# Banded attention on one core: float16 pairs for two more tiles, and score products cut into quadrants of 64 by 64

## The chip, the cores and the metric

The kernel runs on one core of one Trainium2 chip. The metric is device time in microseconds (us) of one execution; less is better. The core has a matrix engine (TensorE, PE in the profile, with its weight loads as PEld), VectorE (DVE), ScalarE (ACT), GpSimd (POOL), SyncE (SP, which issues the DMAs here) and 16 DMA engines.

## The reference

Three stages in a row. Only the first is touched by the change: causal attention with a window of 128 positions and a bias that falls linearly with distance, over 4 batches, 8 heads, 576 positions and head size 64.

```python
scores = scale * np.matmul(q, k.transpose(0, 1, 3, 2))
rel = pos[:, None] - pos[None, :]
bias = slopes[:, None, None] * (-np.abs(rel).astype(np.float32))[None, :, :]
mask = (rel >= 0) & (rel < window)                # window = 128
scores = np.where(mask, scores + bias[None], -1e9)
attn = np.exp(scores - np.max(scores, axis=-1, keepdims=True))
attn = attn / (np.sum(attn, axis=-1, keepdims=True) + 1e-09)
x = np.matmul(attn, v)                            # then to 2304 tokens x 512
h = np.maximum(x @ w_in, 0.0)                     # dense layer, 512 -> 2048 -> 512
x = h * h @ w_out
# then a mixture of 8 experts (512 -> 1024 -> 512), gated by a Sinkhorn iteration
```

## The kernel before, in words

**Tiles.** The 2304 tokens are 18 tiles of 128. Each batch of 576 has four full tiles of 128 positions and 64 left over; the left-overs of two batches make one tail tile. So tiles 0 to 3 and 4 to 7 are full tiles of the first two batches, tile 8 is their tail, and tiles 9 to 17 are the same again. Because the window is 128, a full tile needs its own keys and those of the tile before it (none for tiles 0, 4, 9 and 13). A tail's two halves of 64 queries have different previous tiles.

**One tile of attention.** q and k are transposed on TensorE, so that two heads lie in the two halves of 64 partitions. `scores` multiplies them in float32, two heads (one index j) at a time, from tile 3 on for two values of j in one unit: lines 637 (own keys), 640 (a tail's previous keys, 64 queries at a time) and 642 (a full tile's previous keys). A float32 product shows as two matmul rows, two passes. VectorE adds the bias and takes the maximum (line 651), ScalarE the exponential (line 663). Then the exponentials must be turned before they can be multiplied with the values, and here tiles differ:
- tiles 0 to 8 stay in float32: `turn_e` transposes on TensorE (line 676), ScalarE copies the result back (line 681), `gather` multiplies with the raw values (line 698), two passes a product;
- tiles 9 to 17 (`paired`) are written as a float16 number and a float16 residual: ScalarE casts (`e_hi`, line 550), GpSimd subtracts (`e_lo`, line 437), a DMA transposes (`flip_e`, line 440), and `gather_pairs` makes three float16 matmuls where a float32 one was (line 580). Their values are split in the same way, with a common scale: `v_norm`, `v_sum`, `v_scale`, `v_hi` (line 529), `v_lo` (line 532), and `join_v` (line 545), which rescales a previous tile's values.

**After attention.** Tiles are handed to the dense layer in blocks of 4, 2, 4, 4 and 4. Its products h (line 1037) and y (line 1076) are float16 pairs as well, 96 and 96 matmuls a tile. Its weights come in four groups, which VectorE (lines 901 to 909 and 933) and ScalarE must unpack and split first. The experts follow (lines 1453 and 1548).

**Order.** The program is put in order by a planner (`Plan`): each unit of work has an engine, a cost in us, a rank, what it waits for and what buffers it takes and frees. The planner runs through time and lets each engine take the ready unit of least rank. Attention tiles have ranks by 100 times their number; h and y products have ranks above a million, so on TensorE they fill what attention leaves free. Up to 66 us by the planner's clock, TensorE gets small matmuls that compute nothing (`keep_warm`, line 319) where it has nothing else. GpSimd's units and some of VectorE's (the names in `PORT`, `e_lo` by its engine and `narrow`, `w_lo`, `v_lo` and `join_v` by name) are never planned at the same time, since they share a port. Splitting the values of tiles 9 to 17 (`v_hi`) waits for the first block's y to be done, whose memory it takes over.

Of the kernel before, what the change touches and what calls it, by code (L numbers as in the profile page):

```python
# [15 lines left out]
HI, LO = 0, 1  # L16
# [158 lines left out]
def kernel(  # L175
# [166 lines left out]
    def make_tail():  # L342
# [7 lines left out]

    plan = Plan(
        dict(
            raw=8, qT=2, kT=5, s=1, sp=1, diag=1, e=3, eh=2, eT=3, vo=4, vp=1, av=1, x=1, xh=1, x0=1, x1=1, xb=1, yacc=1,
            h=2, r=2, sq=4, ya=2, y=4, stage=4, scr=1, hp=24, t=10,
        ),
        ("raw", "qT", "kT", "e", "eh", "eT", "vo", "vp", "av", "x", "xh", "stage", "scr", "ya", "y"),
        Model({PE: 0.205, ACT: 0.16, DVE: 0.14, POOL: 0.1}, {PE: 0.0, ACT: 0.135, DVE: 0.115, POOL: 0.12}, 0.065, True),
    )
    GEMM, LATER = -1000000, 1000000
# [33 lines left out]
    def c_act(n, fixed=0.18):  # L393
        return fixed + n * 0.83e-3
# [113 lines left out]
    def v_scale(i):  # L508

        m = main[i]  # L510
        sc = scale_v[i] = small.tile([P, 2], F32, tag="sc", bufs=8, name=f"sc{i}")
        yield from pow2_of_norm((sc[:, 0:1],), m.pop("vss"), 1, WHOLE)
        for x in m["pv"]:
# [5 lines left out]
        for x in m["pv"]:  # L519
            yield  # L520
            f = tiny(1, "fs", bufs=6)
            DVE.tensor_tensor(out=f, in0=scale_v[x][:, 0:1], in1=sc[:, 1:2], op=ALU.mult)
            m["fs"].append(f)

    def v_hi(i):
        if "room" not in values:
            values["room"] = ap_.tile([P, 4, 2, H, D], F16, tag="yacc", name="values")
        values[i] = values["room"][:, plan.got["vo"]]
        ACT.activation(out=values[i][:, HI], in_=raw[i, 2], func=ACTF.Copy, scale=scale_v[i][:, 1:2])

    def v_lo(i):
        DVE.scalar_tensor_tensor(
            out=values[i][:, LO], in0=raw.pop((i, 2)), scalar=scale_v[i][:, 1:2], in1=values[i][:, HI], op0=ALU.mult,
            op1=ALU.subtract,
        )

# [27 lines left out]
    def gather_pairs(i, j):  # L564
        m = main[i]
        if j == 0:
            m["x"] = ps.tile([P, H, D], F32, tag="av", bufs=1, name=f"av{i}")
        eT = m.pop(("eT", j))
        tail = tiles[i][0] == "tail"
        everyone = slice(0, P)  # L570
        for n in range(2):
            h = 2 * j + n
            todo = [(everyone, eT.shape[3] - 1, values[i])]
            if tail:
                todo += [(g, 0, values[x]) for g, x in zip(halves(i), m["pv"])]
            elif m["pv"]:
                todo.append((everyone, 0, m["vp"]))
            for x, (r, c, v_) in enumerate(todo):
                for a, b in PAIRS:
                    PE.matmul(  # L580
                        m["x"][r, h, :], lhsT=eT[:, a, n, c, r], rhs=v_[:, b, h, :], start=x == 0 and a == b,
                        stop=x == len(todo) - 1 and a == LO, skip_group_check=tail,
                    )

    def start(i):
# [34 lines left out]
    def scores(i, js):  # L620

        m = main[i]
        if js[0] == 0:
            m["sum"] = tiny(H, "sum", bufs=3)
            m["nmax"] = tiny(H, "nmax", bufs=3)
        if in_ya(i, js[0]):
            sp = [pa_.tile([P, 512], F32, tag="ya", bufs=2, name=f"s{i}_{js[0]}_{n}") for n in range(2)]
        else:
            sp = pa_.tile([P, 2, 512], F32, tag="sp", bufs=1, name=f"s{i}_{js[0]}")
            sp = [sp[:, n] for n in range(2)]  # L630
        for x, j in enumerate(js):
            at = [sp[n][:, 2 * x * P : 2 * (x + 1) * P] for n in range(2)]
            m["s", j] = at
            for n in range(2):
                r = slice(n * D, (n + 1) * D)
                q_ = m["qT"][r, j]
                PE.matmul(at[n][:, P : 2 * P], lhsT=q_, rhs=keys[i][r, j], start=True, stop=True)  # L637
                if tiles[i][0] == "tail":
                    for g, y in zip(halves(i), m["pv"]):
                        PE.matmul(at[n][g, :P], lhsT=q_[:, g], rhs=keys[y][r, j], start=True, stop=True)  # L640
                elif m["pv"]:
# [41 lines left out]
    def gather(i, j):  # L683
        m = main[i]
        if j == 0:
            m["x"] = ps.tile([P, H, D], F32, tag="av", bufs=1, name=f"av{i}")
        eT = m.pop(("eT", j))
        tail = tiles[i][0] == "tail"
        everyone = slice(0, P)
        for n in range(2):  # L690
            h = 2 * j + n
            todo = [(everyone, eT.shape[2] - 1, i)]
            if tail:
                todo += [(g, 0, x) for g, x in zip(halves(i), m["pv"])]
            elif m["pv"]:
                todo.append((everyone, 0, i - 1))
            for x, (r, c, o) in enumerate(todo):
                PE.matmul(  # L698
                    m["x"][r, h, :], lhsT=eT[:, n, c, r], rhs=raw[o, 2][:, h, :], start=x == 0,
                    stop=x == len(todo) - 1, skip_group_check=tail,  # L700
                )

    done = {}
# [2 lines left out]
    def plan_tile(i):  # L706
# [18 lines left out]
            T.append((t, c))  # L725
        a["kT"], a["v"] = T[1], ld[2]
        jv = None
        if paired(i):
            n = len(pv)
            u = unit(ACT, c_act(W), v_norm, i, rank=z, after=[ld[2], st])  # L730
            mx = unit(
                PE, 0.3, v_sum, i, rank=z, take=["s"], after=[constants["ones"], u, *(done[p]["sc"] for p in pv)]
            )
# [5 lines left out]
            a["v"] = unit(DVE, c_dve(W, 1.17), v_lo, i, rank=z + 11, after=[vh])  # L739
            plan.free(ld[2], "raw", a["v"])  # L740
            if pv:
                older = [] if full else [x for p in pv for x in done[p]["uses"]]
                jv = unit(
                    DVE, 0.43 * n, join_v, i, rank=z + 6, take=["vp"] if full else [],
                    after=[*(done[p]["v"] for p in pv), a["sc"], *older],
                )
        S, X, G = [], [], []
        for j in range(H // 2):
            r = z + 10 * (j + 1)
            js = [j] if i < JOINED else [j, j + 1]  # L750
            if i < JOINED or j % 2 == 0:
                s = unit(
                    PE, 0.26 + 0.24 * nk + 0.9 * (len(pv) > 1) + (0 if i < JOINED else 0.22 * nk + 0.8 * (len(pv) > 1)), scores, i, js, rank=r, take=["ya", "ya"] if in_ya(i, j) else ["sp"],
                    after=[T[0][1], T[1][1], *(done[p]["kT"][1] for p in pv), *S[-1:]],
                )
            b = unit(DVE, 0.27 + 0.265 * nk, bias, i, j, rank=r, take=["e"], after=[s, constants["tail" if len(pv) > 1 else "band"]])
# [2 lines left out]
            if paired(i):  # L759
# [5 lines left out]
                f, cost = gather_pairs, 0.17 * nk + 0.48 * (len(pv) > 1)  # L765
            else:
                t = unit(PE, c_pe(4 * nk, P), turn_e, i, j, rank=r - 5, take=["s", "eT"], after=[x])
                plan.free(b, "e", t)
                c = unit(ACT, c_act(2 * P * nk, 0.07), turned_e, i, j, rank=r - 1, after=[t])
                plan.free(t, "s", c)  # L770
                f, cost = gather, 0.45 * nk
            g = unit(PE, cost, f, i, j, rank=r + 5, take=["av"] if j == 0 else [], after=[c, jv or a["v"], a["v"], *G[-1:]])
            plan.free(t, "eT", g)
            S.append(s)
            X.append(x)
# [2 lines left out]
        for p in (*pv, i):  # L778
            plan.free(done[p]["kT"][0], "kT", *S)
            if not paired(i):  # L780
                plan.free(done[p]["v"], "raw", *G)
            elif full and p != i:
                plan.free(done[p]["vo"], "vo", jv)
            else:
                plan.free(done[p]["vo"], "vo", *G)
        if full and jv:
            plan.free(jv, "vp", *G)
        a["uses"] = [*G, jv]
        z += 80
        st0, _, st = chain(DVE, [TINY, 0.12, 0.62], settle, i, rank=z, take=["x"], after=[*G, *X], port=(0,))  # L790
        plan.free(G[0], "av", st)
        nx = unit(ACT, c_act(W), x_norm, i, rank=z, after=[st])
# [1237 lines left out]
```

## Time and profile before

| | |
|---|---|
| median of 3 runs | 1885.62 us (1885.02 to 1885.77) |
| the profiled execution | 1885.8 us |
| its span, first to last instruction | 1884.0 us |
| mean granted TensorE clock | 0.997 |
| TensorE, VectorE, ScalarE, GpSimd busy | 99%, 80%, 66%, 47% |
| attention | ends at 372 us |

A matmul's row is longer than the array is occupied by it, since matmuls are pipelined: how much of TensorE's time an instruction takes is read from the distance between starts, not from its duration. The granted clock is 1.00 at 2.4 GHz and 0.50 at 1.2 GHz.

### The profile page before, as it was taken

To read this page: it belongs to the slowest core of one execution; us is meant where nothing else is said; L and a number is where in the kernel's file an instruction comes from. 1 tells how busy PE (TensorE), PEld (TensorE's weight loads), DVE (VectorE), ACT (ScalarE), POOL (GpSimd) and SP (SyncE) were. 2 spreads that over 40 slices of the span, in tenths; PEclk is the share of its full clock that TensorE was granted. 3 is DMA by queue.
4 is the path that set the end of the run, shared out by engine and by line. 5 is a ranking of instruction groups with operands and counts; after the bars stand their busy time and mean duration, and the time that the engine had idled before them with its cause. 6 is when DMAs were issued, how large, how long until landed. Compare 5 with 4: busy or idle time off the path is not lost.

```text
span 1884.0 us, 46737 instructions
## 1 busy us (share of the span) xinstructions
PE 1871.5 (99%) x18336; PEld 1676.5 (89%) x18336; DVE 1498.4 (80%) x3853; ACT 1236.2 (66%) x3434; POOL 890.3 (47%) x1182
## 2 busy tenths in 40 slices
PE   9999999999999999999999999999999999999999
PEld 9888888888889899888989989898988988888998
DVE  7996575354358988888898989888898988889876
ACT  6877486354358877666666666666666766666654
POOL 2322345258448744454445544454454535455432
PEclk9999999999999999999999999999999999999999
DMA  9555275110010111010100101010001001000002
GB/s 279 151 143 99 44 114 87 26 52 1 2 46 13 35 35 35 24 35 13 35 24 24 35 23 35 13 35 24 24 24 35 24 24 35 18 30 13 2 24 79
DMA packets 159660, 85.32 MB, mean 45 GB/s; under 512 B 112080, under 2 KB 144848, under 8 KB 159440
## 3 DMA queue, kind: packets, MB, share of 16 engines
q1 hardware_dynamic: 159360, 82.22, 17.4%
q8 instruction: 143, 2.34, 0.5%
q14 instruction: 77, 0.63, 0.1%
q10 hardware_dynamic: 80, 0.13, 0.0%
HBM read 64.50 MB, written 4.72 MB: 37 GB/s over the span
## 4 chain that ended last, share of the span: by engine, by line
PE 88%; DVE 6%; ACT 2%; DMA 2%; issue 1%; POOL 1%; SPq 0%; DVEq 0%; POOLq 0%; ACTq 0%
PE X L1453 19%; PE oX L1548 18%; PE oY L1548 9%; PE Y L1453 9%; PE h L1037 9%; PE y L1076 9%; PE oZ L1548 5%; PE Z L1453 5%; DVE hp L1529 1%; PE s L637 1%; DMA stage<-in_moe_w_dram 1%; PE av L698 1%; PE av L580 1%; PE t L599 1%; DVE acc_wc L1574 1%
## 5 line engine op out<-in xcount | busy, mean ns | idle before, releaser
L1453 PEld LDWEIGHTS <-late 128*128 128x128 f16 x6720 | 617.2, 98 | 71.4 <-issue 5.6
L1548 PEld LDWEIGHTS <-hp 128*128 128x128 f16 x6048 | 583.8, 98 | 64.0 <-issue 0.3
L1548 PE MATMUL oX<-late,hp 128*128 128x256 f16 x3456 | 468.3, 273 | 0.2 <-ACT acc_wd L1569 0.2
L1529 DVE TENSOR_TENSOR hp<-late,hp 128x256 f16<-128x256 f32 (+1 forms) x492 | 228.0, 471 | 21.6 <-ACT hp L1525 18.9
L1453 PE MATMUL Y<-y,late 128*128 128x256 f16 (+1 forms) x1920 | 241.4, 262 | 0.2 <-DVE hp L1508 0.2
L1548 PE MATMUL oY<-late,hp 128*128 128x256 f16 x1728 | 234.4, 273 | 0.0
L437 POOL TENSOR_TENSOR sq<-r,sq 128x256 f16<-128x256 f32 x144 | 107.9, 751 | 249.6 <-ACT sq L1062 245.3
L1525 ACT ACTIVATE hp<-late 128x256 f16<-128x256 f32 (+1 forms) x492 | 193.3, 396 | 46.9 <-POOL late L1515 26.5
L1076 PE MATMUL y<-sq,w_out 128*128 128x256 f16 x1728 | 216.1, 273 | 0.2 <-DVE y L1144 0.2
L1037 PE MATMUL h<-xT,w_in 128*128 128x256 f16 x1728 | 214.9, 274 | 0.3 <-DVE w_in L933 0.3
L1453 PE MATMUL X<-late 128*128 128x256 f16 (+1 forms) x1728 | 204.9, 255 | 2.1 <-ACT late L1481 0.6
L1037 PEld LDWEIGHTS <-w_in 128*128 128x128 f16 x1728 | 169.3, 99 | 21.0 <-DVE w_in L933 0.6
L1076 PEld LDWEIGHTS <-w_out 128*128 128x128 f16 x1728 | 166.9, 98 | 20.2 <-DVE y L1144 0.5
L437 POOL TENSOR_TENSOR stage<-stage 128x256 f32<-128x256 f32 x210 | 160.7, 765 | 34.2 <-DVE late L1353 27.9
L1495 ACT ACTIVATE late<-late 128x256 f32<-128x256 f32 (+1 forms) x202 | 78.5, 393 | 131.5 <-DVE late L1485 129.5
L1353 DVE SCALAR_TENSOR_TENSOR late<-stage,es,late 128x512 f16<-128x512 f32 (+2 forms) x180 | 154.6, 865 | 7.3 <-ACT late L1347 5.9
L1453 PE MATMUL X<-form,late 128*128 128x256 f16 x1152 | 157.1, 272 | 0.4 <-ACT late L1481 0.2
L1529 DVE TENSOR_TENSOR hp<-x,hp 128x256 f16<-128x256 f32 (+1 forms) x308 | 148.9, 489 | 10.7 <-ACT hp L1525 9.1
L1525 ACT ACTIVATE hp<-x 128x256 f16<-128x256 f32 (+1 forms) x308 | 121.7, 397 | 22.4 <-POOL x L1515 12.6
L1347 ACT ACTIVATE late<-stage,es 128x512 f16<-128x512 f32 (+2 forms) x180 | 135.5, 788 | 0.5 <-POOL stage L437 0.3
L1054 DVE SCALAR_TENSOR_TENSOR r<-h,unit_s,r 128x256 f32<-128x256 f32 x96 | 46.2, 482 | 112.3 <-ACT r L1046 112.0
L1515 POOL TENSOR_TENSOR late<-late 128x256 f32<-128x256 f32 (+1 forms) x57 | 45.4, 796 | 186.4 <-DVE hp L1529 178.3
(231 smaller groups left out, 3381.7 us busy)
## 6 DMA issues: line engine op xcount, KB each, us to landing
stage<-in_moe_w_dram SPq DMA_DIRECT2D x60, 256.0 KB, 3.1
stage<-in_moe_w_dram SPq DMA_DIRECT2D x30, 512.0 KB, 3.4
st_in<-in_moe_w_in_dram SPq DMA_DIRECT2D x16, 512.0 KB, 6.6
st_out<-in_moe_w_out_dram SPq DMA_DIRECT2D x16, 512.0 KB, 6.4
raw_q<-in_q_dram SPq DMA_DIRECT2D x16, 256.0 KB, 4.8
raw_k<-in_k_dram SPq DMA_DIRECT2D x16, 256.0 KB, 4.3
raw_v<-in_v_dram SPq DMA_DIRECT2D x16, 256.0 KB, 4.4
out_dram<-acc_wc SPq DMA_DIRECT2D x8, 256.0 KB, 2.2
```

What stands on the lines that cost most here:

```text
L437: POOL.tensor_tensor(out=dst, in0=src, in1=hi, op=ALU.subtract)
L1037: PE.matmul(hp, lhsT=w[:, a, kk, r], rhs=xT[parts1[m][0]][:, b, kk, c : c + MC], start=(kk == 0 and a == b), stop=(kk == KD - 1 and a == LO),)
L1054: DVE.scalar_tensor_tensor(out=r, in0=h if m > 1 else r, scalar=s, in1=r, op0=ALU.mult, op1=ALU.mult)
L1076: PE.matmul(hold["y", m, d // 2][:, d % 2], lhsT=w[:, a, f % FPC, d * P : (d + 1) * P], rhs=sq[:, b], start=(first and d % 2 == 0 and a == ...
L1347: ACT.activation(out=hi, in_=t, func=ACTF.Copy, scale=es[:, g, 2 * kind + 1 : 2 * kind + 2])
L1353: DVE.scalar_tensor_tensor(out=lo, in0=t, scalar=es[:, g, 2 * kind + 1 : 2 * kind + 2], in1=hi, op0=ALU.mult, op1=ALU.subtract)
L1453: PE.matmul(pt, lhsT=w[:, a, row(kk), :], rhs=rhs, start=(x in (1, 2, 5) and kk == 0 and a == c), stop=(x in (2, 3, 4) and kk == KH - 1 an ...
L1495: ACT.activation(out=t, in_=src, func=ACTF.Relu)
L1515: POOL.tensor_tensor(out=c, in0=c, in1=b, op=ALU.add)
L1525: ACT.activation(out=f[:, HI], in_=hold["t", PLACE[name], g, j, p], func=ACTF.Copy)
L1529: DVE.tensor_tensor(out=f[:, LO], in0=hold["t", PLACE[name], g, j, p], in1=f[:, HI], op=ALU.subtract)
L1548: PE.matmul(pt[:, t], lhsT=f[:, a, t * P : (t + 1) * P], rhs=w[:, c, row], start=(x in (1, 2, 5) and p == t == 0 and a == c), stop=(x in ( ...
```

## The change

Four things change. `paired` is also true for tiles 6 and 7, and the values of tile 5, which tile 6 needs as its previous tile, are split too (`valued`); tile 5's own exponentials and tile 8 stay in float32. The split values of these three tiles get two buffers of their own (`vq`) and don't wait for the first block. `scores` makes every product 64 queries by 64 partitions of a head, in the order: own or previous keys, head, half of the queries. And both gathers run over the key tiles outside and the two heads inside. The planner's costs of scores and gathers are adapted.

```diff
-            raw=8, ..., vo=4, vp=1, ...
+            raw=8, ..., vo=4, vq=2, vp=1, ...
...
     PAIRED = 9
+    EARLY = range(6, PAIRED - 1)
     def paired(i):
-        return i >= PAIRED
+        return i >= PAIRED or i in EARLY
+    def valued(i):
+        return paired(i) or any(i in prevs(x) for x in EARLY)
...
     def v_hi(i):
+        if i < PAIRED:
+            values[i] = ap_.tile([P, 2, H, D], F16, tag=f"vq{plan.got['vq']}", name=f"v{i}")
...
     def gather_pairs(i, j):
-        for n in range(2):
-            h = 2 * j + n
-            todo = [(everyone, eT.shape[3] - 1, values[i])]
...
-            for x, (r, c, v_) in enumerate(todo):
+        todo = [(everyone, eT.shape[3] - 1, values[i])]
...
+        for x, (r, c, v_) in enumerate(todo):
+            for n in range(2):
+                h = 2 * j + n
                 for a, b in PAIRS:
...
     def scores(i, js):
-            for n in range(2):
-                r = slice(n * D, (n + 1) * D)
-                q_ = m["qT"][r, j]
-                PE.matmul(at[n][:, P : 2 * P], lhsT=q_, rhs=keys[i][r, j], start=True, stop=True)
-                if tiles[i][0] == "tail":
-                    for g, y in zip(halves(i), m["pv"]):
-                        PE.matmul(at[n][g, :P], lhsT=q_[:, g], rhs=keys[y][r, j], start=True, stop=True)
-                elif m["pv"]:
-                    PE.matmul(at[n][:, :P], lhsT=q_, rhs=keys[i - 1][r, j], start=True, stop=True)
+        for j in js:
+            for c in (P, 0)[: 1 + bool(m["pv"])]:
+                for n, r in enumerate(rows):
+                    for x, g in enumerate(halves(i)):
+                        y = i if c else m["pv"][x % len(m["pv"])]
+                        PE.matmul(
+                            m["s", j][n][g, c : c + P], lhsT=m["qT"][r, j, g], rhs=keys[y][r, j], start=True, stop=True
+                        )
...
     def plan_tile(i):
-        if paired(i):
-            n = len(pv)
+        if valued(i):
+            n = len(pv) if paired(i) else 0
+            vo = "vo" if i >= PAIRED else "vq"
...
-            vh = unit(ACT, c_act(W), v_hi, i, rank=z + 9, take=["vo"], after=[a["sc"], *ready_y[0]])
+            vh = unit(ACT, c_act(W), v_hi, i, rank=z + 9, take=[vo], after=[a["sc"], *(ready_y[0] if i >= PAIRED else ())])
...
-                    PE, 0.26 + 0.24 * nk + 0.9 * (len(pv) > 1) + (0 if i < JOINED else 0.22 * nk + 0.8 * (len(pv) > 1)), scores, ...
+                    PE, 0.26 + 0.217 * nk + (0 if i < JOINED else 0.218 * nk), scores, ...
```

## Rows read from the trace of the kernel before

**Rows 1.** The page's first part: engine, busy us, share of the span, instructions.
```profile
PE 1871.5 (99%) x18336; PEld 1676.5 (89%) x18336; DVE 1498.4 (80%) x3853; ACT 1236.2 (66%) x3434; POOL 890.3 (47%) x1182
```
**Rows 2.** The page's fourth part: the chain that ended last, by engine.
```profile
PE 88%; DVE 6%; ACT 2%; DMA 2%; issue 1%; POOL 1%; SPq 0%; DVEq 0%; POOLq 0%; ACTq 0%
```
**Rows 3.** Stretches: length, busy us (instructions) of PE, PEld, DVE, ACT, POOL; clock, DMA.
```profile
97.00:142.00 45.00, 43.88 (x380) 38.29 (x381) 40.28 (x101) 33.62 (x85) 9.98 (x10) 0.92 0.50 144
...
160.00:210.00 50.00, 49.98 (x476) 44.53 (x474) 23.49 (x87) 27.27 (x83) 17.67 (x24) 1.00 0.44 75
210.00:372.00 162.00, 161.26 (x1769) 140.50 (x1767) 98.40 (x308) 99.29 (x284) 70.55 (x81) 0.99 0.48 79
```
**Rows 4.** TensorE's groups by line, 66 to 160 us: count | busy us, mean ns | idle.
```profile
L1037 PE MATMUL h<-xT,w_in 128*128 128x256 f16 x216 | 28.1, 278 | 0.3 <-DVE w_in L933 0.3
L1076 PE MATMUL y<-sq,w_out 128*128 128x256 f16 x172 | 23.2, 275 | 0.0
```
**Rows 5.** TensorE's timeline in float32 tiles: start, length in us, matmuls merged.
```profile
105.51 0.60 PE L676 MATMUL et<-ident,e 128*128 128x128 f32 x4
...
110.53 2.79 PE L698 MATMUL av<-raw_v,eT 128*128 128x64 f32 x24
113.16 0.33 PE L293 MATMUL total<-wom,ones 128*128 128x1 f32 x2
```
**Rows 6.** TensorE's timeline, gathers of a float16 pair tile; four rows are twelve matmuls.
```profile
234.21 0.25 PE L580 MATMUL av<-values,eT 128*128 128x64 f16 x3
...
234.56 0.36 PE L293 MATMUL total<-vss,ones 128*128 128x1 f32 x2
```
**Rows 7.** TensorE's timeline, one unit of scores (four heads) of a full tile.
```profile
100.37 0.50 PE L637 MATMUL s<-kT,qT 64*128 64x128 f32 x4
100.70 0.40 PE L642 MATMUL s<-kT,qT 64*128 64x128 f32 x4
...
101.14 0.49 PE L642 MATMUL s<-kT,qT 64*128 64x128 f32 x4
101.57 0.83 PE L1076 MATMUL y<-sq,w_out 128*128 128x256 f16 x6
```
**Rows 8.** The same of a tail; the last row shows a 64-column product's second pass alone.
```profile
315.42 0.48 PE L637 MATMUL s<-kT,qT 64*128 64x128 f32 x2
315.83 0.43 PE L640 MATMUL s<-kT,qT 64*64 64x128 f32 x4
...
318.54 0.34 PE L580 MATMUL av<-values,eT 128*128 128x64 f16 x3
...
132.43 0.28 PE L640 MATMUL s<-kT,qT 64*64 64x128 f32 x2
```
**Rows 9.** Stretches as in rows 3, where the clock was low.
```profile
134.20:141.00 6.80, 6.80 (x34) 5.56 (x33) 5.52 (x16) 2.80 (x8) 0.00 (x0) 0.50 0.21 38
...
318.50:321.90 3.40, 3.40 (x36) 2.77 (x35) 1.79 (x8) 1.09 (x4) 1.15 (x2) 0.50 0.66 123
```
**Rows 10.** TensorE's timeline, three gather steps of tail tile 17.
```profile
365.59 2.54 PE L580 MATMUL av<-values,eT 128*128 128x64 f16 x54
```
**Rows 11.** Groups by line and form, 160 to 400 us, of VectorE and GpSimd.
```profile
L532 DVE SCALAR_TENSOR_TENSOR values<-raw_v,sc,values 128x512 f16<-128x512 f32 x9 | 8.4, 940 | 0.1
L545 DVE TENSOR_SCALAR vp<-values,fs 128x1024 f16<-128x1024 f16 x6 | 4.6, 764 | 5.2 <-PE av L580 5.2
...
L437 POOL TENSOR_TENSOR eh<-e,eh 128x512 f16<-128x512 f32 x28 | 33.5, 1204 | 13.1 <-ACT eh L550 10.4 <-PE av L580 1.1 <-PE y L1076 0.9
```
**Rows 12.** Timeline of VectorE and GpSimd: the same instruction beside GpSimd and alone.
```profile
115.71 1.04 POOL L589 TENSOR_TENSOR raw_q<-raw_q,head 128x512 f32<-128x512 f32 x1 [0.98 <-DMA raw_q<-in_q_dram]
...
115.86 1.17 DVE L470 TENSOR_SCALAR xh<-x,xs 128x512 f16<-128x512 f32 x1
...
116.96 0.14 DVE L271 TENSOR_SCALAR out_s<-pn 128x1 f32<-128x1 f32 x1
...
68.22 0.48 DVE L470 TENSOR_SCALAR xh<-x,xs 128x512 f16<-128x512 f32 x1
```

More of the change, by code (lines that the diff above doesn't have):

```diff
@@ L512, in v_scale @@
         yield from pow2_of_norm((sc[:, 0:1],), m.pop("vss"), 1, WHOLE)
-        for x in m["pv"]:
+        pv = m["pv"] if paired(i) else []
+        for x in pv:
             yield
@@ L518, in v_scale @@
         m["fs"] = []
-        for x in m["pv"]:
+        for x in pv:
             yield
@@ L525, in v_hi @@
     def v_hi(i):
-        if "room" not in values:
-            values["room"] = ap_.tile([P, 4, 2, H, D], F16, tag="yacc", name="values")
-        values[i] = values["room"][:, plan.got["vo"]]
+        if i < PAIRED:
+            values[i] = ap_.tile([P, 2, H, D], F16, tag=f"vq{plan.got['vq']}", name=f"v{i}")
+        else:
+            if "room" not in values:
+                values["room"] = ap_.tile([P, 4, 2, H, D], F16, tag="yacc", name="values")
+            values[i] = values["room"][:, plan.got["vo"]]
         ACT.activation(out=values[i][:, HI], in_=raw[i, 2], func=ACTF.Copy, scale=scale_v[i][:, 1:2])
@@ L570, in gather_pairs @@
         everyone = slice(0, P)
-        for n in range(2):
-            h = 2 * j + n
-            todo = [(everyone, eT.shape[3] - 1, values[i])]
-            if tail:
-                todo += [(g, 0, values[x]) for g, x in zip(halves(i), m["pv"])]
-            elif m["pv"]:
-                todo.append((everyone, 0, m["vp"]))
-            for x, (r, c, v_) in enumerate(todo):
+        todo = [(everyone, eT.shape[3] - 1, values[i])]
+        if tail:
+            todo += [(g, 0, values[x]) for g, x in zip(halves(i), m["pv"])]
+        elif m["pv"]:
+            todo.append((everyone, 0, m["vp"]))
+        for x, (r, c, v_) in enumerate(todo):
+            for n in range(2):
+                h = 2 * j + n
                 for a, b in PAIRS:
                     PE.matmul(
-                        m["x"][r, h, :], lhsT=eT[:, a, n, c, r], rhs=v_[:, b, h, :], start=x == 0 and a == b,
-                        stop=x == len(todo) - 1 and a == LO, skip_group_check=tail,
+                        m["x"][r, h, :], lhsT=eT[:, a, n, c, r], rhs=v_[:, b, h, :], start=x == n == 0 and a == b,
+                        stop=x == len(todo) - 1 and a == LO, skip_group_check=True,
                     )
@@ L689, in gather @@
         everyone = slice(0, P)
[L690 to L697, printed above, removed]
+        todo = [(everyone, eT.shape[2] - 1, i)]
+        if tail:
+            todo += [(g, 0, x) for g, x in zip(halves(i), m["pv"])]
+        elif m["pv"]:
+            todo.append((everyone, 0, i - 1))
+        for x, (r, c, o) in enumerate(todo):
+            for n in range(2):
+                h = 2 * j + n
                 PE.matmul(
-                    m["x"][r, h, :], lhsT=eT[:, n, c, r], rhs=raw[o, 2][:, h, :], start=x == 0,
-                    stop=x == len(todo) - 1, skip_group_check=tail,
+                    m["x"][r, h, :], lhsT=eT[:, n, c, r], rhs=raw[o, 2][:, h, :], start=x == n == 0,
+                    stop=x == len(todo) - 1, skip_group_check=True,
                 )
@@ L727, in plan_tile @@
         jv = None
-        if paired(i):
-            n = len(pv)
+        if valued(i):
+            n = len(pv) if paired(i) else 0
+            vo = "vo" if i >= PAIRED else "vq"
             u = unit(ACT, c_act(W), v_norm, i, rank=z, after=[ld[2], st])
             mx = unit(
-                PE, 0.3, v_sum, i, rank=z, take=["s"], after=[constants["ones"], u, *(done[p]["sc"] for p in pv)]
+                PE, 0.3, v_sum, i, rank=z, take=["s"], after=[constants["ones"], u, *(done[p]["sc"] for p in pv[:n])]
             )
@@ L744, in plan_tile @@
                     DVE, 0.43 * n, join_v, i, rank=z + 6, take=["vp"] if full else [],
-                    after=[*(done[p]["v"] for p in pv), a["sc"], *older],
+                    after=[*(done[p]["vl"] for p in pv), a["sc"], *older],
                 )
@@ L752, in plan_tile @@
                 s = unit(
-                    PE, 0.26 + 0.24 * nk + 0.9 * (len(pv) > 1) + (0 if i < JOINED else 0.22 * nk + 0.8 * (len(pv) > 1)), scores, i, js, rank=r, take=["ya", "ya"] if in_ya(i, j) else ["sp"],
+                    PE, 0.26 + 0.217 * nk + (0 if i < JOINED else 0.218 * nk), scores, i, js, rank=r, take=["ya", "ya"] if in_ya(i, j) else ["sp"],
                     after=[T[0][1], T[1][1], *(done[p]["kT"][1] for p in pv), *S[-1:]],
@@ L770, in plan_tile @@
                 plan.free(t, "s", c)
-                f, cost = gather, 0.45 * nk
-            g = unit(PE, cost, f, i, j, rank=r + 5, take=["av"] if j == 0 else [], after=[c, jv or a["v"], a["v"], *G[-1:]])
+                f, cost = gather, 0.45 * nk + 0.05 * (len(pv) > 1)
+            g = unit(PE, cost, f, i, j, rank=r + 5, take=["av"] if j == 0 else [], after=[c, *([jv, a["vl"]] if paired(i) else [a["v"]]), *G[-1:]])
             plan.free(t, "eT", g)
@@ L789, in plan_tile @@
         z += 80
+        if valued(i) and not paired(i):
+            a["v"] = ld[2]
         st0, _, st = chain(DVE, [TINY, 0.12, 0.62], settle, i, rank=z, take=["x"], after=[*G, *X], port=(0,))
```

23 lines of the change are left out of this document (11 added, 12 removed).

## The prediction

> **What bounds the kernel now.** I read the page's busy shares and its chain first: TensorE is busy 99% of the span and 88% of the chain is TensorE [rows 1, 2]. Idle time elsewhere can't be the bound over the whole span; what can be is TensorE's own work, or a stretch in which it is fed by something slower. So the second view is the table by stretch [rows 3]. From 97 to 142 us, where the scores, transposes and gathers of tiles 6 and 7 run, VectorE is busy 40.28 of 45 us and TensorE's granted clock is only 0.92. From 160 us on VectorE falls to 23.49 of 50 us, and from 210 to 372 us, where tiles 9 to 17 are worked on, it is at 98.4 of 162, with TensorE full. There every microsecond that TensorE saves is a microsecond of the end, because the dense layer's h and y products rank behind all attention work and fill whatever attention leaves. Between 66 and 160 us that filler is thinner: 388 of the h and y matmuls run there [rows 4], of 3456 in all for 18 tiles, 192 to a tile and 768 to the block of tiles 0 to 3. The other part of the 768 waits for VectorE's weight splitting. Ahead of 66 us TensorE runs warm-up matmuls when it has nothing else, so savings there are worth nothing.
>
> **Part A, tiles 6 and 7 in float16 pairs.** Removed per tile: 16 transposes and 32 float32 gather passes. Four transposes last 0.60 us of which the last alone is 0.27, so they start 0.11 us apart: 16 make 1.75 us. Twenty-four gather passes start over 2.51 us, 0.109 each: 32 make 3.5 us [rows 5]. Added: 48 float16 matmuls; twelve take 234.21 to 234.56, 0.029 each, so 1.4 us [rows 6]. That is 3.85 us a tile, 7.7 for two. Three sums of the values' squares come in on TensorE at up to 0.33 us with their drain [rows 5], 0.26 as their cadence: 0.8. Part A is 6.9 us, with bounds of 6.5 and 7.5.
>
> **Part B, scores of the two tail tiles.** A tail's unit of four heads runs from 315.42 to 318.54, 3.12 us: products of 128 queries and of 64 alternate, and the array is emptied at each change [rows 8]. After the change its 16 products are all 64 by 64, four for each of the four quadrants of the array, with two passes each: eight starts a quadrant, if the four work side by side. What a start costs: in a full tile's unit the second four heads' half follows the first by 0.44 us for four starts, 0.11 each [rows 7]. So 0.88, and 0.09 to empty the array: 0.97 at the least. At the most it is what a full tile's unit takes now, 100.37 to 101.57, 1.20 us. I take 1.03, near the lower end, because the one start that can't be hidden, the second pass of the first product, follows after 0.16 us in a 64 by 64 product (0.43 less the 0.28 of the last pass) instead of 0.11 [rows 8]. Four units at 3.12 - 1.03: 8.4 us, between 7.7 and 8.6.
>
> **Part C, the clock.** The granted clock is 0.50 from 134.2 to 141.0 and from 318.5 to 321.9 us [rows 9]: 1.2 GHz instead of 2.4. Both falls come during or right behind a tail's unit of scores, the first at 134.2 in the middle of one, the second at the end of the one of rows 8; between 160 and 372 us, with 12 such units, these 3.4 us are all that keeps the mean from 1.00 [rows 3]. Ten microseconds at half speed cost 5.1. With tail units made like full ones I expect both falls gone: 5.1 us, at worst 0.
>
> **Part D, scores of the other tiles.** A unit with a previous tile goes from 1.20 to 1.03 by the working of part B, 0.17. There are 18 such units behind 66 us (tiles 5 to 7, 10 to 12, 14 to 16, two each), and four smaller ones (tiles 9 and 13) at less than half that: 3.4 us. The lower bound is 0 if all four quadrants side by side are no faster than two row halves, the upper 4.5 at 0.97; a loss is the second and third rival below. The trace shows two row halves at once (four passes of line 637 begin within 0.33 us) and two column halves at once (rows of line 640), never four quadrants.
> The row also says that starts aren't in the program's order: the source gives one head's own and previous products (lines 637, 642) and then the next head's, yet the four passes of line 637 begin ahead of the first of line 642 [rows 7]. The Trainium skill says the opposite ("TensorE: Matmul & The Clock Gate", Part 3, The mechanism): matmuls start and end strictly in program order. By the row a unit is 1.03 us; by the rule, with one quadrant's two passes 0.16 apart and in line, it would be 2.7, and the change a loss; that is the third rival.
>
> **Part E, gather order in the tails.** 54 tail matmuls of three steps take 2.54 us, 0.85 a step [rows 10], against 18 at 0.029, 0.52: 0.33 for four changes between 128 and 64 columns. Two of four go: 0.16 a step, four steps, two tails: 1.3 us, bounds 0 and 1.5.
>
> **Part F, what VectorE and GpSimd get.** VectorE gets three value residuals at 0.94, two rescalings at 0.76 and 13 one-column instructions at 0.14: 6.1 us [rows 11, 12], and its slack from 97 to 142 us is 4.7 [rows 3]. GpSimd gets eight residuals of exponentials at 1.20, and beside a GpSimd instruction a VectorE one took 1.17 us that alone takes 0.48 [rows 11, 12]: 0 to 5.5 us for eight of them. To fill TensorE's freed 15 us with h and y, VectorE must also make some six more squares of 256 elements, by half the length of the 512-element rows at most 3 us. So it is over by 1 to 10 us just where it feeds TensorE, and queued behind it are the splits of the last two weight groups, for which the h and y filler waits. On ScalarE the copies of turned exponentials are replaced by casts of the same size, and eight DMA transposes go into SP's queue ahead of weight loads; the DMA share there is 0.50 [rows 3], so I cost them at nothing while loads are early, and at part of F's upper end if not. TensorE has filler of the second weight groups to bridge some of this. I take a loss of 5 us, about the middle of 1 to 10. No reason excludes a larger one: the whole of what is saved ahead of 160 us.
>
> **The sum.** 6.9 + 8.4 + 5.1 + 3.4 + 1.3 = 25.1, less 5: 20.1. The profiled execution took 1885.8 us (span 1884.0 and 1.8 around it), and the median of the runs shown is 1885.62, so the two are interchangeable. 1885.8 - 20.1 = 1865.7: I say **1866**.
>
> **Rivals.**
> First, VectorE takes TensorE's place from 66 to 160 us, and all that is saved there (part A, tile 8's halves of B and E, the first clock fall, tiles 5 to 7 of D) turns into waiting. What is left is the second half: 4.2 + 1.7 + 0.65 + 2.2 = 8.8, that is 1877. For it: 40.28 of 45 us. Against: 380 of block 0's h and y matmuls, less those ahead of 66 us, are still to come at 160, so there is work to pull forward.
> Second, only two of four quadrants run at once: sixteen starts at 0.11 and the emptying, 1.85 us a unit. 18 units lose 11.7, four small ones 1.4, the tails gain 5.1; with A, E and F (6.9 + 1.3 - 5) the rest is a loss of 4.8 if the clock still falls and a gain of 0.3 if not: 1885.5 to 1891, no change or a little slower. Against: both kinds of halves overlap in the rows.
> Third, the slower side: the passes start in program order, quadrant by quadrant. Place: every unit of scores. Price: 16 products at 0.16 and 0.1 to empty, 2.7 us against 1.20; 18 units lose 27, four small ones 3.3, the tails gain 1.7, A, E and F give 3.2 back: 25.4 slower, 1911. It decides from a unit of about 1.7 us on (1.9 if the clock stays up). For it: nothing but the rule; against it: rows 7.
> Fourth, as forecast, but the clock goes on falling behind the tails or in a new wait: 1871; this lies in the forecast's range.
>
> **How the numbers follow.** Forecast (1858 to 1873): 0.62. More than that, under 1858 (F near nothing): 0.05. First rival and what lies between (1873 to 1882): 0.17. Second: 0.07 within 0.2% and 0.03 beyond. Third, with anything else slower: 0.06. A measurement of this kernel can tell about 0.2%, 3.8 us, from no change. So faster 0.84, same 0.07, slower 0.09. The range of 1856 to 1881 holds the forecast, some of what is faster and nearly all of the first rival's 0.17: 0.8.
>
> **What would show it.** A full tile's unit of scores, start to next start: 1.0 to 1.1 us right, 1.2 no gain, 1.7 and more a loss. The tails' units the same length. Granted clock 1.00 from 97 to 160 us. TensorE's float32 transposes fewer by 32 and gathers by 64. TensorE's idle time from 97 to 160 us under 5 us, and h products of the last weight groups not held by the weights' split (line 933 in the waits); if they are, the first rival. The second half, from the start of tile 9's values to the end, should be some 9 us shorter whatever happens ahead of it; if it isn't, the reading of parts B and D is wrong.

## The result and the profile after

The change takes 1867.8 us (median of 4 runs, 1866.62 to 1868.23) against 1885.69 for the kernel before: a ratio of 0.9906, with a 95% interval of 0.9891 to 0.992. The profiled execution took 1867.95 us, its span is 1866.2.

The page's first part, TensorE's own line, and the chain by engine, to be laid beside [rows 1, 2]:

```profile
PE 1847.5 (99%) x18834; PEld 1653.4 (89%) x18834; DVE 1503.3 (81%) x3871; ACT 1238.5 (66%) x3443; POOL 902.1 (48%) x1190
...
PE 86%; DVE 6%; ACT 3%; DMA 3%; issue 1%; POOL 1%; SPq 0%; DVEq 0%; ACTq 0%; POOLq 0%
```

This line already holds the balance. TensorE is busy 1871.5 - 1847.5 = 24.0 us less. Its idle time, span less busy, went from 1884.0 - 1871.5 = 12.5 to 1866.2 - 1847.5 = 18.7 us, 6.2 more. The difference, 17.8, is what the span lost. The forecast had 25.1 and 5.

TensorE's timeline shows a full tile's unit of scores, then a tail's, then the gathers of tile 6 (start, length in us, matmuls merged, in brackets idle time and what ended it); [rows 6 to 8] are the counterparts:

```profile
80.89 1.10 PE L647 MATMUL s<-kT,qT 64*64 64x128 f32 x32
81.93 2.14 PE L1047 MATMUL h<-xT,w_in 128*128 128x256 f16 x18
...
147.65 1.10 PE L647 MATMUL s<-kT,qT 64*64 64x128 f32 x32
148.69 0.83 PE L1086 MATMUL y<-sq,w_out 128*128 128x256 f16 x6
...
129.53 0.34 PE L588 MATMUL av<-v,eT 128*128 128x64 f16 x6
...
130.58 0.82 PE L1047 MATMUL h<-xT,w_in 128*128 128x256 f16 x6
```

Both kinds of units last 1.04 us from their start to the next operation's. Tile 6's gathers, 36 matmuls from 129.53 to 130.58, come at 0.029 us each. That four products run side by side is seen when the same timeline is cut to 0.1 us around a unit's begin: four matmuls of 0.32 us lie within 0.34.

```profile
80.89 0.34 PE L647 MATMUL s<-kT,qT 64*64 64x128 f32 x4
```

The table by stretch (length, busy us and instructions of PE, PEld, DVE, ACT, POOL, then clock and DMA), as [rows 3]:

```profile
66.00:97.00 31.00, 30.34 (x319) 26.88 (x316) 29.71 (x77) 26.23 (x69) 10.77 (x12) 1.00 0.64 179
97.00:142.00 45.00, 42.69 (x531) 37.03 (x531) 41.82 (x100) 34.95 (x89) 21.85 (x20) 1.00 0.87 189
142.00:160.00 18.00, 17.29 (x179) 14.94 (x178) 16.18 (x50) 14.45 (x38) 7.52 (x9) 1.00 0.45 72
160.00:372.00 212.00, 210.16 (x2656) 184.19 (x2655) 134.71 (x435) 135.67 (x388) 88.23 (x104) 1.00 0.47 89
372.00:1866.00 1494.00, 1483.35 (x14278) 1331.98 (x14275) 1229.41 (x3043) 977.89 (x2727) 757.89 (x1016) 1.00 0.08 26
```

The clock is 1.00 in all of these stretches; the two falls of [rows 9] are gone. TensorE's idle time in them is 0.7, 2.3, 0.7, 1.8 and 10.7 us; the same cuts before give 0.8, 1.1, 0, 0.8 and 8.4. The warm-up is to be added, with 2.3 us after and 1.4 before. Here is the warm-up after, then the warm-up and the last stretch before:

```profile
0.00:66.00 66.00, 63.71 (x883) 58.38 (x884) 51.50 (x169) 49.31 (x136) 15.89 (x31) 1.00 0.92 225
...
0.00:66.00 66.00, 64.60 (x750) 59.86 (x751) 52.93 (x168) 48.97 (x133) 17.85 (x32) 1.00 0.93 225
372.00:1884.00 1512.00, 1503.57 (x14531) 1352.00 (x14529) 1240.70 (x3080) 987.44 (x2752) 761.98 (x1023) 1.00 0.09 27
```

Between 66 and 160 us it is hardly VectorE that TensorE waits for (one wait of 0.3 us names it). TensorE's longest waits over the whole span, in total, times, longest:

```profile
PE Y L1463 <- DVE hp L1518: 2.1, 2, 1.5
PE av L588 <- DMA eT<-eh: 1.3, 2, 1.1
PE warm L319 <- DVE slope L308: 1.1, 1, 1.1
PE h L1047 <- DMA xT<-xh: 1.0, 1, 1.0
PE total L293 <- ACT junk L428: 1.0, 1, 1.0
```

The first stands at the experts' beginning (559 us). The second stands mostly at a turned exponential of tile 6 (137 us), the third and fourth in the first 66 us, and the fifth at the squares of a value tile on ScalarE (134 us). ScalarE had itself waited 1.42 us for the load of those values, so both waits of about 1 us between 97 and 142 us lead back to a DMA:

```profile
133.54 0.63 ACT L428 ACTIVATE junk<-raw_v 128x512 f16<-128x512 f32 x1 [1.42 <-DMA raw_v<-in_v_dram]
```

In that stretch the DMA engines' busy share went from 0.50 [rows 3] to 0.87, and a transposed exponential took 5.6 us from issue to landing (the last figure, a median of six):

```profile
eT<-eh SPq DMA_TRANSPOSE x6, 5.6
```

### The profile page after: what moved, and what is told of

Its sections match the earlier page's. It is cut to its first block, busy times and chain, and to the rows that moved or that the text cites. A ratio compares the mean times of both kernels' runs of the same rounds, so it can differ in the third digit from the quotient of the medians.

```text
span 1866.2 us, 47775 instructions
## 1 busy us (share of the span) xinstructions
PE 1847.5 (99%) x18834; PEld 1653.4 (89%) x18834; DVE 1503.3 (81%) x3871; ACT 1238.5 (66%) x3443; POOL 902.1 (48%) x1190
## 3 DMA queue, kind: packets, MB, share of 16 engines
q1 hardware_dynamic: 167808, 84.32, 18.2%
## 4 chain that ended last, share of the span: by engine, by line
PE 86%; DVE 6%; ACT 3%; DMA 3%; issue 1%; POOL 1%; SPq 0%; DVEq 0%; ACTq 0%; POOLq 0%
PE X L1463 19%; PE oX L1558 18%; PE oY L1558 9%; PE Y L1463 9%; PE h L1047 8%; PE y L1086 8%; PE oZ L1558 5%; PE Z L1463 5%; DVE hp L1539 2%; PE s L647 2%; DMA stage<-in_moe_w_dram 1%; PE warm L319 1%; PE av L588 1%; PE t L607 1%; DVE acc_wc L1584 1%
## 5 line engine op out<-in xcount | busy, mean ns | idle before, releaser
L1086 PEld LDWEIGHTS <-w_out 128*128 128x128 f16 x1728 | 166.6, 98 | 22.6 <-issue 3.2
L1535 ACT ACTIVATE hp<-x 128x256 f16<-128x256 f32 (+1 forms) x308 | 121.4, 396 | 21.8 <-POOL x L1525 12.6
```

Source lines behind the costliest of these rows:

```text
L1086: PE.matmul(hold["y", m, d // 2][:, d % 2], lhsT=w[:, a, f % FPC, d * P : (d + 1) * P], rhs=sq[:, b], start=(first and d % 2 == 0 and a == ...
L1535: ACT.activation(out=f[:, HI], in_=hold["t", PLACE[name], g, j, p], func=ACTF.Copy)
```

## Experiments

Each run is compared with the kernel before, measured beside it on the same chip: 1883.2 us for e1, e2, e9 and e4, 1883.6 for e12, e10, e11 and e6, and 1883.9 for the others. Busy and idle are TensorE's, from each run's page. For the kernel before they are 1871.5 and 12.5, from its own profile of 1885.8 us with a mean clock of 0.997; beside the experiments its mean clock was 0.997 to 0.999. So differences of busy time from the kernel before can be too large by some 2 us, while those between the experiments don't have this fault.

| run | median us | less than before | ratio, interval | busy | idle |
|---|---|---|---|---|---|
| scores only (e1) | 1870.97 | 12.2 | 0.9935, 0.9919 to 0.9952 | 1855.3 | 14.0 |
| pairs only (e2) | 1875.71 | 7.5 | 0.9958, 0.9944 to 0.9973 | 1860.8 | 11.3 |
| all but pairs (e9) | 1867.67 | 15.5 | 0.9917, 0.9903 to 0.9932 | 1853.3 | 12.4 |
| full tiles whole (e4) | 1862.43 | 20.8 | 0.9888, 0.9874 to 0.9903 | 1848.3 | 12.8 |
| the change again (e12) | 1864.89 | 18.8 | 0.9901, 0.9887 to 0.9916 | 1846.3 | 16.8 |
| other planner costs (e10) | 1861.72 | 21.9 | 0.9879, 0.9862 to 0.9895 | 1846.2 | 14.8 |
| full tiles whole, the change's order (e11) | 1864.80 | 18.8 | 0.9901, 0.9886 to 0.9916 | 1849.9 | 13.2 |
| quadrant after quadrant (e6) | 1895.37 | -11.7 | 1.0062, 1.0047 to 1.0077 | 1881.0 | 12.2 |
| tails whole (e3) | 1873.57 | 10.4 | 0.9944, 0.9928 to 0.9961 | 1859.7 | 14.2 |
| old gather order (e5) | 1866.60 | 17.3 | 0.9910, 0.9895 to 0.9924 | 1848.1 | 16.4 |
| measured unit costs (e13) | 1862.04 | 21.9 | 0.9887, 0.9872 to 0.9902 | 1845.2 | 14.4 |
| tile 5 too (e14) | 1870.47 | 13.5 | 0.9929, 0.9914 to 0.9944 | 1846.9 | 21.8 |

### One part at a time

Scores only: the kernel before with the change's `scores` and its planner cost.

> The kernel before with the new score products alone: no pairs in tiles 6 and 7, gathers as before. If the terms of the forecast add up and only the pairs load VectorE and GpSimd (theory 1), the scores bring 8.4 (tails) + 5.1 (clock) + 3.4 (other tiles) = 16.9: 1868.8 us, with idle time on TensorE as before. If TensorE simply has too little to fill with ahead of 160 us, whatever it is that makes it faster (theory 2), a part of this goes into idle time here too: about 1873.

Pairs only: the change with the `scores` and both gathers of before, and their costs.

> The change without the new score products and without the new gather order: only tiles 6 and 7 as float16 pairs. Theory 1 (the pairs alone load VectorE and GpSimd and so cause all of the idle time that came in): 6.9 saved on TensorE, some 4 to 6 given back, 1880 to 1884 us, with 3 us or more of new idle time ahead of 160 us. Theory 2 (too little filler, whoever saves): less is saved here, so less turns idle, about 1880. The clock still falls twice, at the tails.

All but the pairs:

```diff
-    EARLY = range(6, PAIRED - 1)
+    EARLY = range(0)
```

> The change without the pairs of tiles 6 and 7 (they stay in float32): new score products and new gather order. Theory 1: 1868.8 less 1.3 for the gather order, 1867.5, so the pairs bring next to nothing of their own in the whole change, since what they save they give back. Theory 2: the pairs still bring some 4 to 5 us, so this run is at 1872 to 1873.

The expectations gave times for a kernel before of 1885.7 us, so their distances from it are what to compare. Scores only: 16.9 below by theory 1, some 13 by theory 2, measured 12.2. Pairs only: 2 to 6 by theory 1, 6 by theory 2, measured 7.5. All but the pairs: 18.2 by theory 1, some 13 by theory 2, measured 15.5. Neither theory gives all three.

Theory 1 falls by the pairs-only run, in which TensorE is idle no more than before (11.3 against 12.5 us). The pairs by themselves load no engine that TensorE waits for. TensorE is busy 10.7 us less there, but this holds one fall of the clock less than before: ahead of the run's last 3 us the clock is low from 135.6 to 139.0 us only, 3.4 us instead of 10.2. At half speed that is 3.4 of the 10.7, and the 7.3 left are near part A's 6.9. Without the pairs, too, TensorE's idle time is near that of before (12.4 and, with the scores alone, 14.0). Under the change's order the new idle time comes only with both, 16.8 to 18.7. The gains of 7.5 and 15.5 add up to 23, and the whole brings 18 to 19.

### The full tiles' score products

Full tiles as before, tails in quadrants:

```diff
     def scores(i, js):
+        if tiles[i][0] != "tail":
+            return scores_whole(i, js)     # the function of the kernel before
...
-    PE, 0.26 + 0.217 * nk + (0 if i < JOINED else 0.218 * nk), scores
+    PE, 0.26 + (0.24 if len(pv) < 2 else 0.217) * nk + (0 if i < JOINED else (0.22 if len(pv) < 2 else 0.218) * nk), scores
```

> The change, but full tiles' score products are whole again (128 queries), and only the tails' are cut into quadrants. If a full unit gains 0.17 us (18 of them after the warm-up, four smaller ones), 3.4 us are lost against the change: 1871. If the gain on full tiles is hidden, 1868. The clock should not fall, if it was the tails' mixed units that made it fall; if it is the width of all score products, it falls again.

This came out under both expectations: 20.8 below before, with little idle time and no fall of the clock, as it was to be if the tails' mixed units made it fall. Two things differ from the change, the products and the order that the planner writes when it is given other costs. The next three runs part them.

> The change itself again, to stand beside the others on the same chip: 17.9 us below the kernel before, whatever the chip.

Other planner costs: the change with the second line of the diff above alone.

> The change with the planner's costs of a full tile's score unit left at the old ones (0.24 and 0.22 for each key tile instead of 0.217 and 0.218). The work is the change's, every product in quadrants; only the order that the planner writes differs. Theory 3 (the loss of some 5 us of idle time in the change is an accident of its order): this order is the one of the run with whole full tiles, which had little idle time, so the quadrants' 3.4 to 4 us come on top of its 20.8: 24 us below the kernel before. Theory 2 (too little to fill with): as the change, 18 below.

Full tiles whole with the change's order: the first part of that diff alone.

> Full tiles' score products whole as in the earlier run, but in the order that the planner writes for the change. Theory 3: the idle time belongs to this order, so it is slower than the earlier run of the same work (20.8 below the kernel before) by some 4 to 5 us: 14 to 17 below. Theory 2: slower products leave less to idle away, so about 20 below again.

Under the change's order, quadrants in full tiles bring nothing: 1864.89 and 1864.80 us on one chip, though TensorE is 3.6 us less busy (1849.9 - 1846.3). Three cuts of these two show where it goes (in the fourth, 160 to 372 us, they differ by 0.1). First full tiles whole, then the change again:

```profile
372.00:1863.00 1491.00, 1482.82 (x14284) 1334.11 (x14281) 1230.09 (x3043) 977.32 (x2728) 758.13 (x1016) 1.00 0.08 26
0.00:66.00 66.00, 64.65 (x754) 59.87 (x755) 52.82 (x169) 49.12 (x136) 15.10 (x31) 1.00 0.88 225
66.00:160.00 94.00, 91.86 (x935) 80.77 (x933) 88.25 (x228) 76.43 (x194) 41.35 (x40) 1.00 0.69 164
```

```profile
372.00:1863.00 1491.00, 1480.78 (x14260) 1331.87 (x14257) 1227.70 (x3041) 975.44 (x2724) 758.43 (x1016) 1.00 0.08 26
0.00:66.00 66.00, 63.69 (x884) 58.19 (x885) 51.67 (x169) 49.32 (x136) 15.75 (x31) 1.00 0.91 225
66.00:160.00 94.00, 91.10 (x1034) 79.98 (x1032) 87.26 (x229) 76.70 (x196) 42.06 (x40) 1.00 0.71 164
```

Idle time is up by 1.0 us in the warm-up, 0.8 from 66 to 160 and 2.0 behind 372, together the 3.6. The 2.0 is mostly one wait at the experts' beginning, for a residual of VectorE's, which the run with whole full tiles doesn't have:

```profile
557.14 0.50 PE L1463 MATMUL Y<-y,late 128*128 128x128 f16 x6 [1.55 <-DVE hp L1518]
```

Under the other order the quadrants' full tiles are at 21.9 below (e10) and whole ones at 20.8 (e4); the intervals overlap, so a gain of about 1 us there is not shown. The measured distances lie between the two expectations each time: e10's 21.9 between 24 and 18, e11's 18.8 between 14 to 17 and 20. And the order alone moves the change's own work from 18.8 to 21.9 below: the runs of e12 (1864.19 to 1866.83) and e10 (1859.34 to 1862.76) don't overlap, while the intervals of their ratios just do. Both theories hold a part: some 3 us hang on the planner's order, and what the full tiles save finds little to fill.

One part of what an order does is seen from 97 to 142 us. In the change, e12, e11, e3 and e5 a transposed exponential took 5.1 to 5.8 us to land there (medians), and TensorE idled for 1.2 to 2.3 us. In e10, e4, e2 and e13 it took 3.2 to 3.9 us, and TensorE idled for 0 to 0.5 us. The line of e10, to be laid beside the 5.6 above:

```profile
eT<-eh SPq DMA_TRANSPOSE x5, 3.5
```

The two go together in these nine runs, and not in the other two with pairs: e6 has 5.3 us and no idle time there, e14 3.5 us and 2.4 of idle time. That the later landing makes the idle time is shown in the change for one wait of 1.1 us; no run changed the transposes alone.

### Who starts when in the array

The products of a unit, quadrant after quadrant:

```diff
-        for j in js:
-            for c in (P, 0)[: 1 + bool(m["pv"])]:
-                for n, r in enumerate(rows):
-                    for x, g in enumerate(halves(i)):
+        for n, r in enumerate(rows):
+            for x, g in enumerate(halves(i)):
+                for j in js:
+                    for c in (P, 0)[: 1 + bool(m["pv"])]:
```

> The change with the score products issued quadrant after quadrant: each quadrant's four products (eight passes) stand together in the program, and the next quadrant's follow. If each quadrant has a queue that looks far enough ahead, the unit stays at 1.03 us and the time at the change's. If passes start in the program's order, the change would have shown it already; if the look-ahead is shorter than a quadrant's sixteen instructions, a unit grows towards four quadrants in a row: 4 times 0.16 + 7 times 0.11, some 3.7 us, and with 22 units 50 us and more are lost.

A unit grows from 1.04 to 2.50 us, between the 1.03 and the 3.7 of the expectation, and 30 us against the change are lost:

```profile
106.95 2.56 PE L647 MATMUL s<-kT,qT 64*64 64x128 f32 x32
109.45 0.50 PE L1086 MATMUL y<-sq,w_out 128*128 128x256 f16 x3
```

Cutting the timeline shows how. Up to 107.438 us five passes have started, one behind the other; 12 ns on there are six:

```profile
106.95 0.76 PE L647 MATMUL s<-kT,qT 64*64 64x128 f32 x5
...
106.95 0.81 PE L647 MATMUL s<-kT,qT 64*64 64x128 f32 x6
```

The rows don't name a pass or its quadrant, but passes of one quadrant follow at 0.109 us, so the sixth start belongs to another one: the second quadrant's first pass, ninth in the program. It overtakes three waiting ones, and no more. In [rows 7] the second head's first pass overtook three as well, and in the change the fourth quadrant's overtakes three (the second passes of the other quadrants). Neither an endless look-ahead nor the program's order holds: it lies between. With, by these starts, two quadrants at most in work, a unit of 2.50 us is beyond the second rival's 1.85 and near the third's 2.7, and past the 1.7 from which the forecast had the change lose.

### The tails and the clock

The change with the tails' products and their planner cost as before:

```diff
     def scores(i, js):
+        if tiles[i][0] == "tail":
+            return scores_whole(i, js)
```

> The change, but the two tails' score products as before: 128 queries for their own keys, 64 for the previous ones, in turns. If the tails' units are worth 2.09 us each and all of it reaches the end, 8.4 us are lost against the change; and if their mixed units make the clock fall, it falls again, once or twice, for 1.7 to 3.4 us each: 10 to 13 us slower than the change, some 6 to 9 below the kernel before. If the tails' gain was hidden behind other engines, less than 4 us are lost.

It is 10.4 below before, where the change again was 18.8: 8.4 us, less than the 10 to 13 expected and more than the 4 of a hidden gain. In the profiled execution the clock fell twice, for 10.2 and 3.4 us:

```profile
135.20:145.50 10.30, 10.30 (x58) 6.96 (x57) 6.46 (x15) 7.29 (x16) 5.65 (x6) 0.50 0.69 98
312.70:316.10 3.40, 3.40 (x34) 2.60 (x31) 1.66 (x8) 1.09 (x4) 0.62 (x1) 0.50 0.74 113
```

The first fall began at 135.2, ahead of the tail's first unit (136.0) and behind a wait of TensorE of 1.7 us; the tail's unit then ran under it:

```profile
134.68 0.38 PE L293 MATMUL total<-vss,ones 128*128 128x1 f32 x2 [1.73 <-ACT junk L428]
...
136.02 0.79 PE L645 MATMUL s<-kT,qT 64*128 64x128 f32 x2
```

So a tail's mixed unit isn't the only thing behind which the clock falls. At half speed the 13.6 us cost TensorE up to 6.8 of the 13.4 us that it was busier than in the change again. But the profiled execution is the slowest of its four, at a mean clock of 0.996; the others have 0.998, so the clock's share of the 8.4 is smaller, and its size stays open. TensorE's idle time is 2.6 us lower in exchange.

### Gather order, and two attempts at more

> The change with both gathers in the old order (heads outside, key tiles inside) and the planner's old costs for them. By the forecast's part E 1.3 us are lost on TensorE: four changes of width a step instead of two, at 0.08 each, in eight steps of two tails. The planner's order differs a little, so the time may be 1 to 3 us off either way; TensorE's occupation by gathers is what counts: 1.3 us more.

TensorE is busy 1.8 us more than in the change again, and the time moves by about as much (17.3 against 18.8 below), within what the intervals allow. On the row itself, three gather steps of tile 17 take 2.54 us in this order (at 346.57) and 2.09 in the change's (at 345.39): 0.15 a step, 1.2 us for the eight steps of two tails if tile 8's gain as much.

The planner's costs at the length that the trace shows:

```diff
-    PE, 0.26 + 0.217 * nk + (0 if i < JOINED else 0.218 * nk), scores
+    PE, 0.26 + 0.2 * nk + (0 if i < JOINED else 0.185 * nk), scores
```

> The change with the planner given the score units' length as the trace of the change shows it: 1.03 us for a unit with a previous tile (0.2 and 0.185 for each key tile instead of 0.217 and 0.218). The work is the change's. If the lost time in the change is an accident of its order, a third order comes out anywhere between the two seen so far (19 and 22 below the kernel before); if a plan with the truer cost is the better one, at 22 or more below.

21.9 below, with 14.4 us idle: as good as the other costs. Together with e10 it is the best of what ran, 3 us under the change. That is still one of the times that an accident of the order would give, so the better cost isn't shown to be the reason.

Tile 5 as well, on top of the other planner costs (e10):

```diff
-    EARLY = range(6, PAIRED - 1)
+    EARLY = range(5, PAIRED - 1)
```

> The order that did best so far (old planner's costs for full tiles' scores, 21.9 below the kernel before) with tile 5 as float16 pairs too, and so the values of tile 4. TensorE saves another 3.5 us in the stretch where VectorE is fullest. If there is filler left for it, some 24 to 25 below the kernel before; if the stretch ahead of 160 us is now bound by VectorE, the saving turns idle and it stays at 20 to 22.

13.5 below, under both expectations and 8.4 us worse than the same planner costs without tile 5. Here the first rival is to be seen. VectorE is busy 17.72 of 18 us from 142 to 160, TensorE idles for 21.8 us in all, and it waits for VectorE and its followers:

```profile
PE s L647 <- DVE nmax L658: 2.1, 2, 1.9
PE et L683 <- ACT eT L688: 1.6, 2, 0.9
PE t L607 <- DVE pn L266: 1.5, 1, 1.5
```

The clock falls behind such waits, at 159.8 for 3.4 us and at 166.6 for 6.8 us, with no mixed unit near. The waits ahead of the two falls, and the stretches:

```profile
158.42 0.34 PE L588 MATMUL av<-v,eT 128*128 128x64 f16 x6 [1.04 <-DVE x L450]
...
165.37 0.67 PE L647 MATMUL s<-kT,qT 64*64 64x128 f32 x16 [1.93 <-DVE nmax L658]
```

```profile
142.00:160.00 18.00, 16.37 (x218) 14.68 (x220) 17.72 (x47) 11.54 (x25) 4.41 (x3) 0.99 0.46 75
...
166.60:173.40 6.80, 5.34 (x34) 3.90 (x35) 4.79 (x19) 6.26 (x22) 3.60 (x5) 0.50 0.01 2
```

At half speed the 10.2 us cost up to 5.1 us, more than the 3.5 that tile 5 was to save; with 7.0 us more of idle time than e10 has, this is where the gain went.

## Why the prediction was right, step by step

1866 was forecast and 1867.8 measured, and the two totals behind it were right as well: 25.1 us off TensorE's work (24.0 measured), 5 lost to new idle time (6.2). That the loss came out near 5 was partly luck: it didn't come where or why the forecast had it, part D's saving brought nothing under this order, and two other orders of the same work lose only about 2.

One of the forecast's own signs shows this. From the start of the first value split of tiles 9 to 17 (221.5 us before, 206.9 after) to the end was to be some 9 us shorter. Nearly the same h and y products are left at the two points (2530 and 2534 matmuls), but the rest is only 3.3 us shorter, with 6.6 us less of TensorE's busy time and 3.3 more of idle time:

```profile
221.50:1884.00 1662.50, 1653.33 (x16192) 1482.19 (x16189) 1329.95 (x3367) 1081.27 (x3024) 830.42 (x1100) 1.00 0.13 32
...
206.90:1866.10 1659.20, 1646.77 (x16372) 1474.98 (x16369) 1330.47 (x3367) 1082.14 (x3024) 830.77 (x1100) 1.00 0.12 32
```

The other 14.6 us were gained ahead of it, where the forecast had put the loss. The forecast would have had this mean that its reading of parts B and D is wrong. The lengths of the units are as it read them; what doesn't hold is that behind 160 us all of it reaches the end.

- **Part A** (6.9): the run without pairs and the two of the change differ by 5.8 and 7.0 us of TensorE's busy time. In the end the pairs bring 3.3 us on top of the other parts (18.8 in e12 against 15.5 in e9). The pair gathers came at the 0.029 us of [rows 6].
- **Part B** (8.4): a tail's unit is 1.04 us, 1.03 was forecast; four times 3.12 - 1.04 is 8.3. In the end parts B and C together, forecast at 13.5, were worth 8.4 (e3 against e12), with the clock not falling in one and falling in the other.
- **Part C** (5.1): both falls are gone. That the tails' units cause them was too simple: with tails in quadrants the clock also fell, in the run with tile 5, behind idle time. In the other nine profiled kernels with tails in quadrants, with 12.2 to 18.7 us idle, it fell only in the last 3 us of the run. The 12 units between 160 and 372 us that the forecast mentions are the full tiles'; of tails' units there are two.
- **Part D** (3.4): the saving on TensorE is there. A full tile's unit went from 1.20 to 1.04 us, a little less than forecast, and e11 and e12 differ by 3.6 us of busy time, 1.0 of it in the warm-up, which the forecast left out. As a gain in the end it was wrong: under the change's order it is 0, under the other one not more than about 1. The step that failed is "every microsecond that TensorE saves is a microsecond of the end". It doesn't hold behind 160 us either, where 2 of the 3.6 turned into idle time behind 372 us, most of it in one wait at the experts' beginning.
- **Part E** (1.3): 1.2 us by the gathers' rows, 1.8 us of busy time in all.
- **Part F** (a loss of 5): right in size, wrong in place and cause. It was to be VectorE's and GpSimd's new work from 97 to 142 us. VectorE is only 1.5 us fuller there (41.82 against 40.28 of 45), and the pairs by themselves cost no idle time. Of the 6.2 us, 0.9 are in the warm-up, 1.7 between 66 and 160 and 3.3 behind it; the rest is at the very end. The longest wait behind it is for VectorE's residuals for the experts, at 559 us. The waits from 97 to 142 us lead to the term that part F put at nothing, the DMA transposes and the loads around them. Part of the loss is the planner's order: two other orders of the same work have 14.4 and 14.8 us of idle time instead of 18.7, or 16.8 in e12. Of part F's row prices two were too high, a value residual at 0.74 us in that stretch instead of 0.94 and a rescaling at 0.48 instead of 0.76. GpSimd's residual of exponentials was too low, with 1.35 instead of 1.20.
- **The rivals.** The first did not happen in the change, and did with one tile more. The second and third were rightly set aside for the change's order of products. The third's mechanism is real in a weaker form: had the products been written quadrant after quadrant, the change would have lost 11.7 us to the kernel before. The rule cited for it from the Trainium skill ("TensorE: Matmul & The Clock Gate", Part 3, The mechanism: starts in program order) does not agree with these traces, in which a pass starts ahead of up to three that stand before it.

What stays open: why two orders of the same work differ by some 3 us was followed to the idle time and, from 97 to 142 us, to later landings that go with it, not to one cause; and the clock's share in the tails' gain was not measured by itself.

## What to carry to other kernels

In sum, prices on the bound engine, taken from start to start, were good to 5% of what that engine saved; what of it reaches the end is another question, to be asked again for each consumer downstream, also far behind the edit. Here the tails (mixed widths, 3.12 us a unit) were worth 8.4 us with the clock's part, and the full tiles, whose products ran two side by side before, at most about 1. Where a planner writes the order, run the same work under two or three cost tables before an edit worth under 0.2% is called good or bad. For matmuls on quadrants, alternate the quadrants within the program so that no start has to overtake more than three waiting ones.

## What the runs showed of the hardware

Four 64 by 64 float32 products ran side by side: four starts within 0.02 us, and a unit of 32 passes in 1.04 us (the change). A pass for an idle row half or quadrant overtook three waiting passes and no more, in three different programs (before, the change, e6). The granted clock fell from 1.00 to 0.50 for 6.8 us behind a wait of TensorE of 1.93 us (e14, at 166.6). It also fell for 6.8 us in the middle of a unit of mixed widths (before, at 134.2), in which TensorE was busy 6.80 of 6.80 us. And a DMA transpose of an exponential took 3.2 to 5.8 us to land from 97 to 142 us (medians of the profiled runs with pairs).
